# Reordering the start of a spectral-mixing and shrink kernel: early function table, copies first in the second unit, conversion and constant products in a gap

## Chip, cores, metric

One core of a Trainium2 chip. The metric is device time in microseconds (us) of one execution. Executions of the same kernel scatter by about 3 to 5 us on either side of the median, and the effects studied here are 1 to 12 us out of 2840. No run was slow by the record's rule (over 1.5% above the fastest of its kernel); one single look has no state. The experiments ran in three later calls on three chips, so runs of different calls are compared by their ratios to the kernel before, which ran in the same rounds. So most conclusions rest on two things together: the timed runs, and stretches of the trace between two fixed instructions, which repeat to a tenth of a us where nothing in them depends on DMA or on the clock.

## The reference

```python
# attention block: x (8, 3008, 256), filt_r, filt_i (1505, 256)
X = np.fft.rfft(x, axis=1)
y = np.fft.irfft(X * (filt_r + 1j * filt_i)[None], n=3008, axis=1)
# expert block on the 24064 x 256 result; w_in (256, 2048), w_out (2048, 256)
h = y.reshape(-1, 256) @ w_in
g = h - np.tanh(h)
out = g @ w_out
```

The weights arrive as 64-bit floats and are rebuilt as 32-bit floats with integer steps ("conversion" below).

## The kernel before

The Fourier transform is split over units of one or two batches. A prologue does unit 0 alone. The main loop then runs steps U = 0, 1, 2, ...: `up(U)` makes the seven products of a 2x2 block scheme with w_in (numbers 1 to 7 in `mm`), `shrink(U-1)` the activation on ScalarE and VectorE, `down(U-2)` the seven products with w_out; transforms of the next unit (`pf`, `pz`, `pe`) are strewn between. `pu` is the last product of a transform; ScalarE copies it to `ut`, and `up` works on `ut` and on `tu`, sums that GpSimd makes from it. The products of `up` go into three banks x, y, z (tiles that TensorE writes), those of `down` into four; a bank can be written anew once its copy is made. The program fixes the order by hand, and ScalarE's list in the prediction runs in it, so the order in this code is the order of each queue.

```python
def converted(tiles, src, dsts, queue, alone=False):      # one job: 128 x 512 numbers
    ...
    V.tensor_scalar(out=it, ...); V.tensor_scalar(out=pt, ...); V.tensor_scalar(out=st, ...)
    yield
    if alone:      # two steps on VectorE
        V.tensor_scalar(out=ft, ...); V.tensor_scalar(out=pt, ...)
    else:          # the same two on ScalarE
        ACT.activation(ft, it, AF.Identity, ...); ACT.activation(pt, pt, AF.Relu, bias=exp_b)
    yield
    ...            # three more steps and the writes of wu / wd, all on VectorE

# the prologue's end (tiles in the pools "pro" and "ps0", which are closed after it)
back0()                                   # last product pe and copy e1s, stored
for _ in range(EARLY): next(fs)           # two pf products, copies "a"
load_e2(*groups[0], e2s[0], slice(48, 64))
for _ in ws: pass                         # rest of quarters 3..5 of the weights
# ... then, in the main pools "dn" and "ps":
late = weights_slow(tiles1, range(6, 8))  # quarters 6 and 7 of the weights, inside the loop
for _ in last(0, z1): pass                # pu products, copies ut (a tile of "dn")

def up(U, d, e, s, t):      # d, e: steps of down; s: one of shrink; t: transforms, conversion
    mm(X, 1, True); mm(Y, 2, True)
    s1 = copied("s1")                     # ScalarE reads bank x
    t(0); d(); s()
    V.tensor_add(h[:, 0, :, 0:w], Y, s1)
    e(); s(); s(); t(1)
    mm(X, 6, False); mm(Z, 5, True)
    u2 = copied("u2")                     # ScalarE reads bank x; the next mm(X) waits for it
    d(); s(); e(); t(2)
    mm(X, 7, False)
    u3 = copied("u3")
    ...
# shrink: six steps: arctan+square, square with bias, end; the same for the other half
```

Of the kernel before, what the change touches and what calls it, by code (L numbers as in the profile page):

```python
# [9 lines left out]
F32 = mybir.dt.float32  # L10
# [4 lines left out]
AF = mybir.ActivationFunctionType  # L15
# [47 lines left out]
A, B = 0.18659689165196622, -0.6846325776203513  # L63
# [80 lines left out]
def kernel(  # L144
# [9 lines left out]
    nc = tc.nc  # L154
    V, G, ACT = nc.vector, nc.gpsimd, nc.scalar
# [11 lines left out]
    cst = ctx.enter_context(tc.tile_pool(name="cst", bufs=1))  # L167
# [97 lines left out]
    def begun(tiles, job, alone=False):  # L265
        j = converted(tiles, *job, nc.sync, alone)
        next(j)
        return j

    def weights(tiles, quarters, ahead):  # L270


        jobs = parts_of(quarters)
        began = [begun(tiles, job) for job in jobs[:ahead]]
        yield
        for k in range(len(jobs) + 1):
            if k < len(jobs):
                next(began[k])
            if k > 2 and k % 2:
                sums(quarters[k // 2 - 1])  # L280
            yield
            if k < len(jobs):
                next(began[k])
            if k > 0:
                for _ in began[k - 1]:
                    pass
            if k + ahead < len(jobs):
                began.append(begun(tiles, jobs[k + ahead]))
            yield
        sums(quarters[-1])  # L290
        yield

    def weights_alone(tiles, quarters):

        jobs = parts_of(quarters)
        began = [begun(tiles, job, True) for job in jobs[:2]]
        yield
        for k in range(len(jobs)):
            if k + 2 < len(jobs):
                began.append(begun(tiles, jobs[k + 2], True))  # L300
            for _ in began[k]:
                pass
            if k % 2:
                sums(quarters[k // 2])
            yield

    def weights_slow(tiles, quarters):

        jobs = parts_of(quarters)
        began = [begun(tiles, job) for job in jobs[:2]]  # L310
        yield
        for k in range(len(jobs)):
            for _ in began[k]:
                yield
            if k + 2 < len(jobs):
                began.append(begun(tiles, jobs[k + 2]))
            if k % 2:
                sums(quarters[k // 2])
                yield
# [212 lines left out]
    def up(U, d, e, s, t):  # L532

        i, u = divmod(U, 4)
        b, tu, w = uts[i]
        rhs = [b[0][0], b[1][0], b[1][1], tu[:, 3, 0:w], tu[:, 0, 0:w], tu[:, 1, 0:w],
               tu[:, 2, 0:w]]
        banks = {k: ps.tile([128, 2, 256], F32, tag=k, bufs=1, name=k) for k in "xyz"}
        X, Y, Z = (banks[k][:, :, 0:w] for k in "xyz")
        h = dn.tile([128, 4, 2, 256], F32, tag="h", bufs=3, name="h")  # L540
        hs[U] = (h, w)

        def mm(bank, q, first):
            for k in range(2):
                nc.tensor.matmul(bank[:, k], wu[:, q - 1, (2 * u + k) * 128:(2 * u + k + 1) * 128],  # L545
                                 rhs[q - 1], start=(first and k == 0), stop=True,
                                 skip_group_check=True)

        def copied(tag):
            t = dn.tile([128, 2, 256], F32, tag=tag, bufs=1, name=tag)[:, :, 0:w]  # L550
            ACT.copy(t, X)  # L551
            return t


        mm(X, 1, True)
        mm(Y, 2, True)
        s1 = copied("s1")
        t(0)
        d()
        s()  # L560
        V.tensor_add(h[:, 0, :, 0:w], Y, s1)  # L561
        e()
        s()
        s()
        t(1)
        mm(X, 6, False)
        mm(Z, 5, True)
        u2 = copied("u2")
        d()
        s()  # L570
        e()
        t(2)
        mm(X, 7, False)
        u3 = copied("u3")
        V.tensor_add(h[:, 3, :, 0:w], Z, u3)  # L575
        d()
        s()
        e()
        t(3)
        mm(X, 4, False)  # L580
        V.tensor_copy(h[:, 2, :, 0:w], X)  # L581
        s()
        d()
        e()
        t(4)
        mm(Z, 3, False)
        V.tensor_add(h[:, 1, :, 0:w], Z, u2)

    def shrink(U):

# [158 lines left out]
    def bounded(z):  # L749


        small = tr.tile([128, 2 * 4 * len(groups)], F32, tag="a2", bufs=2, name="small")
        ones = cst.tile([128, 1], F32, name="ones")
        least = cst.tile([128, 1], F32, name="least")
        G.memset(ones, 1.0)
        V.tensor_single_scalar(out=small, in_=y_sums, scalar=float(np.arctan(S * NEAR) ** 2),
                               op=ALU.is_lt)
        V.tensor_reduce(out=least, in_=small, axis=mybir.AxisListType.X, op=ALU.min)
        pc = z("pc", [1, 1])
        nc.tensor.matmul(pc, least, ones, start=True, stop=True)  # L760
        V.tensor_copy(count, pc)
# [69 lines left out]
    with tc.tile_pool(name="tr", bufs=2) as tr, tc.manual_schedule():  # L831
        with tc.tile_pool(name="pro", bufs=1) as pro, \
                tc.tile_pool(name="ps0", bufs=6, space=bass.MemoryType.PSUM) as ps0:

            def z0(name, shape):
                return ps0.tile(shape, F32, tag="z", bufs=6, name=name)
# [7 lines left out]
            def load_x0(c, cuts=(0, 8)):  # L844
                t = big([128, 8, DM], F32, "x0")
                for lo, hi in zip(cuts, cuts[1:]):
                    for h, rows, r, n in halves(0, 8 * c + lo, hi - lo):
                        (nc.sync, ACT)[h].dma_start(
                            t[rows, lo:lo + n, :],
                            dram(x.tensor, r * DM, [[NR * DM, 64], [1, n * DM]]))  # L850
                return t
# [60 lines left out]
            V.memset(near_b, B)  # L912
            V.memset(exp_b, -896.0)
            xs = [load_x0(0, (0, 4, 8)), load_x0(1), load_x0(2)]
            ws = weights_alone(tiles0, range(3))

            pad = pro.tile([64, DM], F32, name="pad")
# [48 lines left out]
            for j in range(NK // 2):  # L966
                c = j // 2
                if j % 2 == 0 and c + 1 < NK // 4:
                    if c + 2 < NK // 4:
                        a2[c + 2] = load_a2(0, c + 2, False, ("a2", "ft")[c % 2])  # L970
                        mats[c + 2] = load_slots(c + 2, pro)
                        fts[c + 2] = filters_of(c + 2)
                pz = z0("pz", [128, 2, DM])
                for i in range(2):
                    k = (2 * j + i) % 4
                    nc.tensor.matmul(pz[:, i], mats[c][0][0:R2, k],
                                     a2[c][0:R2, k * DM:k * DM + DM], start=True, stop=True)
                if waiting:
                    back0()
                uv = tr.tile([128, 2, DM], F32, tag="uv", bufs=2, name="uv")  # L980
                zs = tr.tile([128, 2, DM], F32, tag="zs", bufs=2, name="zs")
                ft = fts[c][:, :, j % 2 * 2:j % 2 * 2 + 2]
                V.tensor_mul(uv, pz, ft[:, 0])
                V.tensor_mul(zs, pz, ft[:, 1])
                waiting.append((j, uv, zs))
                next(ws, None)
                if j % 2 and c + 1 < NK // 4:
                    double_filters(fts[c + 1], c + 1)
                    turned(mats[c + 1][1], gx[(c + 1) % 2])
                if j == NK // 2 - 3:  # L990
                    fs = first(1, z1)
                    next(fs)
                if j == NK // 2 - 1:
                    e2s[0] = load_e2(*groups[0], None, slice(0, 48))
            back0()
            for _ in range(EARLY):
                next(fs)
            load_e2(*groups[0], e2s[0], slice(48, 64))
            for _ in ws:
                pass  # L1000


        with tc.tile_pool(name="dn", bufs=2) as dn, \
# [32 lines left out]
                                     [[2 * NK * DM, m], [DM, n], [1, DM]]), src)  # L1036
                    yield

            late, copies = weights_slow(tiles1, range(6, 8)), filters_d()
            total = 4 * len(groups)  # L1040
            for _ in last(0, z1):
                pass
# [1 line left out]
            for U in range(total + 2):  # L1044
# [27 lines left out]
                def d():  # L1072

                    next(dw, None)
# [5 lines left out]
                def s():  # L1080

                    next(sh, None)
# [26 lines left out]
                if U < total:  # L1109
                    if U == total - 1:  # L1110
                        one = tr.tile([128, 128], F32, tag="x", bufs=3, name="one_sb")
                        nc.sync.dma_start(one, one_d)
                    up(U, d, e, s, t)
                else:
                    for k in range(5):
                        s()
                        s()
                        d()
                        e()
                        t(k)  # L1120
                        if U == total + 1 and k == 0:
                            bounded(z1)
# [39 lines left out]
```

## Time and profile before

| | before |
|---|---|
| median of 6 runs | 2841.91 us (2837.63 to 2843.91) |
| span of the profiled run | 2839.5 us, granted clock 0.986 |
| TensorE busy | 96% of the span |
| TensorE busy from 114 to 170 us | 41.6 of 56 us |

The prediction shows the lines that matter: the slices, the windows from 114 to 222 us, TensorE's waits and ScalarE's queue in U=1. The windows' columns are start:end, length, busy us of TensorE, its weight loads, VectorE, ScalarE and GpSimd (with instruction counts), granted clock, share of the DMA engines, GB/s. In a timeline line the columns are start, duration, engine, line, operation, output<-inputs, sizes, count, and in brackets the idle time just before with what ended it.

### The profile page before, as it was taken

Reading aid. Unit: us, or ns where it says so; the run is one execution under the profiler, and the core shown is the slowest. Engines: PE = TensorE matmul, PEld = TensorE weight load, DVE = VectorE, ACT = ScalarE, POOL = GpSimd, SP = SyncE. Lnnn points to the kernel's source line nnn. Section 1 sums busy time; section 2 is a strip of 40 time slices with the busy share of each in tenths; the row PEclk is TensorE's granted clock in tenths of the full one; section 3 lists DMA queues with packets and bytes.
Section 4 is the critical chain, followed back from the end, with each engine's and each line's share of the span. In section 5 each row is a group of like instructions: output and inputs, shape, how many; then the busy total and the mean of one; then the engine's idle time right before and its main releaser. Section 6 shows DMA issues by size and latency. Waiting matters only on the chain.

```text
span 2839.5 us, 36615 instructions
## 1 busy us (share of the span) xinstructions
PE 2734.4 (96%) x12418; PEld 2270.6 (80%) x12418; DVE 1910.9 (67%) x2170; ACT 1881.9 (66%) x2794; POOL 1794.4 (63%) x1407
## 2 busy tenths in 40 slices
PE   4799999999999999999999999999999999999998
PEld 2567777988877787888877787788888888898887
DVE  6565665666766677656666776676676767677776
ACT  2476666666767766666666667666676676667665
POOL 5456887544677767744577776755466667656555
PEclk7899999999999999999999999999999999999999
DMA  9754443232233322232332223212222322101010
GB/s 251 199 184 104 116 107 85 69 104 72 67 80 77 79 70 60 48 90 79 73 94 67 70 71 79 54 41 65 63 65 61 79 55 53 34 17 27 16 22 17
DMA packets 322592, 217.53 MB, mean 77 GB/s; under 512 B 224782, under 2 KB 274746, under 8 KB 322156
## 3 DMA queue, kind: packets, MB, share of 16 engines
q1 hardware_dynamic: 266826, 157.28, 23.6%
q10 hardware_dynamic: 52818, 51.53, 6.0%
q0 software_dynamic: 2752, 6.30, 0.9%
q8 instruction: 100, 1.64, 0.3%
q14 instruction: 96, 0.79, 0.1%
HBM read 138.87 MB, written 79.17 MB: 77 GB/s over the span
## 4 chain that ended last, share of the span: by engine, by line
PE 77%; ACT 9%; issue 5%; DVE 4%; POOL 1%; ACTq 1%; DMA 0%; DVEq 0%; SPq 0%; POOLq 0%
PE o L653 31%; PE x L545 20%; PE z L545 9%; PE y L545 5%; PE pe L411 3%; PE pu L511 3%; ACT y L601 3%; PE pz L430 3%; PE pf L351 2%; DVE h L607 1%; ACT u L551 1%; ACT zs L444 1%; ACT y L602 1%; DVE uv L445 1%; ACT zs L443 1%
## 5 line engine op out<-in xcount | busy, mean ns | idle before, releaser
L653 PE MATMUL o<-t,wd 128*128 128x256 f32 (+2 forms) x3072 | 776.2, 375 | 1.8 <-POOL t L526 1.3
L607 DVE TENSOR_TENSOR h<-h,y 128x1024 f32<-128x1024 f32 (+2 forms) x384 | 570.4, 1485 | 279.6 <-ACT y L602 279.6
L653 PEld LDWEIGHTS o<-t,wd 128*128 128x128 f32 x3072 | 580.7, 190 | 74.2 <-POOL t L526 1.6
L545 PE MATMUL x<-tu,wu 128*128 128x256 f32 (+2 forms) x2304 | 589.1, 378 | 15.4 <-ACT u L551 15.1
L653 PE MATMUL o<-h,wd 128*128 128x256 f32 (+2 forms) x2304 | 582.4, 375 | 0.2 <-DVE h L611 0.2
L611 DVE SCALAR_TENSOR_TENSOR h<-sq,h 128x1024 f32<-128x1024 f32 (+2 forms) x384 | 566.7, 1476 | 20.5 <-ACT y L601 0.5
L524 POOL TENSOR_TENSOR t<-h 128x512 f32<-128x512 f32 (+2 forms) x192 | 240.6, 1253 | 501.6 <-DVE h L611 443.9
L545 PEld LDWEIGHTS x<-tu,wu 128*128 128x128 f32 x2304 | 427.8, 190 | 159.1 <-issue 73.1
L653 PEld LDWEIGHTS o<-h,wd 128*128 128x128 f32 x2304 | 431.2, 190 | 71.3 <-issue 18.8
L608 ACT ACTIVATE sq<-y,near_b 128x1024 f32<-128x1024 f32 (+2 forms) x384 | 435.6, 1134 | 5.0 <-DVE h L611 0.2
L601 ACT ACTIVATE y<-h 128x1024 f32<-128x1024 f32 (+2 forms) x384 | 400.0, 1042 | 14.8 <-ACT e L414 8.0
L602 ACT ACTIVATE y<-y 128x1024 f32<-128x1024 f32 (+2 forms) x384 | 399.2, 1040 | 12.2
L551 ACT COPY s<-x 128x512 f32<-128x512 f32 (+2 forms) x192 | 110.9, 577 | 443.2 <-PE x L545 431.7
L527 POOL TENSOR_TENSOR t<-t,h 128x512 f32<-128x512 f32 (+2 forms) x192 | 308.0, 1604 | 0.1
L551 ACT COPY u<-x 128x512 f32<-128x512 f32 (+2 forms) x384 | 219.2, 571 | 55.6 <-PE x L545 21.9
L525 POOL TENSOR_TENSOR t<-h,t 128x512 f32<-128x512 f32 (+2 forms) x192 | 241.3, 1257 | 15.1
L526 POOL TENSOR_TENSOR t<-h 128x512 f32<-128x512 f32 (+2 forms) x191 | 248.2, 1299 | 0.0
L575 DVE TENSOR_TENSOR h<-z,u 128x512 f32<-128x512 f32 (+2 forms) x192 | 129.5, 674 | 171.1 <-ACT u L551 168.2
L446 POOL TENSOR_TENSOR zs<-zs,ft 128x512 f32<-128x512 f32 x112 | 166.1, 1483 | 103.5 <-ACT zs L444 103.4
L447 POOL TENSOR_TENSOR uv<-uv,zs 128x512 f32<-128x512 f32 x112 | 213.7, 1908 | 14.0 <-DVE uv L445 5.5
L545 PE MATMUL x<-ut,wu 128*128 128x256 f32 (+2 forms) x768 | 199.2, 382 | 4.8 <-DVE h L581 3.0
L561 DVE TENSOR_TENSOR h<-y,s 128x512 f32<-128x512 f32 (+2 forms) x192 | 130.2, 678 | 106.0 <-PE y L545 87.7
(119 smaller groups left out, 3389.4 us busy)
## 6 DMA issues: line engine op xcount, KB each, us to landing
a<-ct SPq DMA_DIRECT2D x64, 384.0 KB, 4.2
ft<-filt SPq DMA_DIRECT2D x96, 256.0 KB, 4.3
out_dram<-ot SPq DMA_DIRECT2D x1392, 16.0 KB, 1.5
ct<-e ACTq DMA_DIRECT2D x112, 192.0 KB, 2.4
ct<-a ACTq DMA_DIRECT2D x80, 256.0 KB, 2.9
x_sb<-in_x_dram SPq DMA_DIRECT2D x69, 256.0 KB, 2.9
e<-ct SPq DMA_DIRECT2D x33, 512.0 KB, 4.3
fg<-fg SPq DMA_DIRECT2D x40, 392.0 KB, 6.2
```

What stands on the lines that cost most here:

```text
L524: G.tensor_sub(t[0], b[0][1], b[0][0])
L525: G.tensor_sub(t[1], b[1][1], t[0])
L526: (V if shared else G).tensor_sub(t[2], b[1][1], b[0][1])
L527: G.tensor_sub(t[3], t[1], b[1][0])
L545: nc.tensor.matmul(bank[:, k], wu[:, q - 1, (2 * u + k) * 128:(2 * u + k + 1) * 128], rhs[q - 1], start=(first and k == 0), stop=True, ski ...
L551: ACT.copy(t, X)
L601: ACT.activation(y[k], ht[k], AF.Arctan, scale=S)
L602: ACT.activation(y[k], y[k], AF.Square, accum_out=y_sums[:, 2 * U + k // 2:2 * U + k // 2 + 1])
L607: V.tensor_mul(ht[k], ht[k], y[k])
L608: ACT.activation(sq[k], y[k], AF.Square, bias=near_b, scale=A)
L611: V.scalar_tensor_tensor(out=ht[k], in0=sq[k], scalar=K, in1=ht[k], op0=ALU.add, op1=ALU.mult)
L653: nc.tensor.matmul(product(q), wd[:, q - 1, (2 * u + k) * 128: (2 * u + k + 1) * 128], rhs[q - 1][:, k], start=(u == 0 and k == 0 and q == ...
```

## The change

Its intent is to take out what TensorE waits for between the prologue and the steady loop. Five parts: (1) the function table for arctan loaded at the start; (2) in U=1 the copies u2 and u3 ahead of the shrink steps; (3) quarter 6 of the weights (the third of w_out's four) converted in the gap after the prologue, quarter 7 on VectorE alone; (4) ten constant products in the gap; (5) the vector of ones for the last check made ready early.

```diff
@@ weights_slow: all jobs with alone=True
-        began = [begun(tiles, job) for job in jobs[:2]]
+        began = [begun(tiles, job, True) for job in jobs[:2]]
@@ up: the fixed s() calls become shrinks(k), k = 0..7, after the same places
+        steps_at = ([1, 2, 0, 1, 0, 1, 1, 0] if U > 1 else [0, 0, 1, 0, 2, 0, 1, 2])
+        def shrinks(at):
+            for _ in range(steps_at[at]):
+                s()
   (places 2 and 4 are new: right after copy u2, and after copy u3 and its add)
@@ bounded
-        ones = cst.tile([128, 1], F32, name="ones")
-        G.memset(ones, 1.0)
@@ prologue
             xs = [load_x0(0, (0, 4, 8)), load_x0(1), load_x0(2)]
+            ACT.activation(near_b, near_b, AF.Arctan)
+            V.memset(near_b, B)
@@
                     fs = first(1, z1)
                     next(fs)
+                    ws_gap = weights(tiles0, range(6, 7), 2)
+                    next(ws_gap)
@@
-            for _ in ws:
-                pass
+            for w in (ws, ws_gap):
+                for _ in w:
+                    pass
+            warm = z0("warm", [128, 2, 128])
+            for _ in range(10):
+                nc.tensor.matmul(warm, wf1[:, 0], wf1, start=True, stop=True)
@@
-            late, copies = weights_slow(tiles1, range(6, 8)), filters_d()
+            late, copies = weights_slow(tiles1, range(7, 8)), filters_d()
@@ last unit
+                        ones = cst.tile([128, 1], F32, name="ones")
+                        G.memset(ones, 1.0)
```

More of the change, by code (lines that the diff above doesn't have):

```diff
@@ L315, in weights_slow @@
             if k + 2 < len(jobs):
-                began.append(begun(tiles, jobs[k + 2]))
+                began.append(begun(tiles, jobs[k + 2], True))
             if k % 2:
@@ L559, in up @@
         d()
-        s()
+        shrinks(0)
         V.tensor_add(h[:, 0, :, 0:w], Y, s1)
         e()
-        s()
-        s()
+        shrinks(1)
         t(1)
@@ L568, in up @@
         u2 = copied("u2")
+        shrinks(2)
         d()
-        s()
+        shrinks(3)
         e()
@@ L575, in up @@
         V.tensor_add(h[:, 3, :, 0:w], Z, u3)
+        shrinks(4)
         d()
-        s()
+        shrinks(5)
         e()
@@ L581, in up @@
         V.tensor_copy(h[:, 2, :, 0:w], X)
-        s()
+        shrinks(6)
         d()
@@ L587, in up @@
         V.tensor_add(h[:, 1, :, 0:w], Z, u2)
+        shrinks(7)
     def shrink(U):
```

## The prediction

> **What bounds the kernel now.** I read the 40 slices first, then a table of windows, then the per-engine timelines of the first 260 us.
>
> The slices:
>
> ```profile
> PE   4799999999999999999999999999999999999998
> PEclk7899999999999999999999999999999999999999
> ```
>
> TensorE is at 90% or more from the third slice of 71 us on, so the body is TensorE-bound and any time gained in front of it moves its start forward. Only the first two or three slices and the last have anything to gain. The windows between 114 and 222 us (start:end, length, then busy us of each engine, granted clock, DMA):
>
> ```profile
> 114.00:126.00 12.00, 5.36 (x20) 3.76 (x19) 1.19 (x3) 2.34 (x4) 0.73 (x1) 0.68 0.90 249
> 126.00:138.00 12.00, 10.89 (x39) 7.59 (x39) 4.68 (x10) 5.13 (x9) 2.86 (x4) 0.89 0.50 147
> 138.00:158.00 20.00, 14.50 (x43) 9.92 (x44) 12.50 (x19) 12.91 (x18) 5.16 (x6) 0.74 0.66 208
> 158.00:170.00 12.00, 10.81 (x45) 8.11 (x44) 9.48 (x14) 10.02 (x15) 5.29 (x6) 1.00 0.66 213
> 170.00:222.00 52.00, 52.00 (x227) 41.67 (x226) 33.75 (x43) 33.82 (x52) 29.55 (x29) 1.00 0.51 155
> ```
>
> From 114 to 170 us TensorE is busy 41.6 of 56 us, part of that at a clock of 0.68 to 0.89; from 170 on it is busy without a break. So the target of the change is those 56 us: the gap between prologue and main loop, and units U=0, 1, 2. Their waits on TensorE, from its timeline (start, duration, idle before it):
>
> ```profile
> 121.94 2.05 PE L511 MATMUL pu<-s_sb,e 128*128 128x128 f32 x8 [5.92 <-DMA e<-ct]
> 124.70 2.07 PE L511 MATMUL pu<-s_sb,e 128*128 128x128 f32 x8 [0.72 <-ACT ut L513]
> 126.57 1.91 PE L545 MATMUL x<-ut,wu 128*128 128x256 f32 x4
> 148.22 2.08 PE L545 MATMUL x<-tu,wu 128*128 128x256 f32 x4 [4.96 <-ACT u L551]
> 158.61 1.89 PE L653 MATMUL o<-h,wd 128*128 128x256 f32 x8
> 166.00 1.13 PE L545 MATMUL x<-tu,wu 128*128 128x256 f32 x4 [1.19 <-ACT u L551]
> ```
>
> Elsewhere the same eight pu instructions take 0.89 and four x instructions 0.86 us (chain of work, from 170 us on); here 2.07 and 1.71. These are half-clock matmuls after an idle. The 4.96 us wait belongs to U=1: the copy u2, which frees the x bank, stands on ScalarE behind this:
>
> ```profile
> 140.71 0.59 ACT L352 COPY a<-pf 128x512 f32<-128x512 f32 x1 [1.14 <-PE pf L351]
> 141.33 0.37 ACTq L353 DMA_DIRECT2D ct<-a  x1
> 141.74 0.63 ACT L216 ACTIVATE ft<-it 128x512 f32<-128x512 int32 x1 [0.44 <-ACT a L352]
> 142.28 0.70 ACT L217 ACTIVATE pt<-pt,exp_b 128x512 int32<-128x512 int32 x1
> 142.99 1.28 ACT L601 ACT_TABLE_LOAD   x1
> 144.28 1.06 ACT L601 ACTIVATE y<-h 128x1024 f32<-128x1024 f32 x1
> 145.37 1.06 ACT L602 ACTIVATE y<-y 128x1024 f32<-128x1024 f32 x1
> 146.55 1.15 ACT L608 ACTIVATE sq<-y,near_b 128x1024 f32<-128x1024 f32 x1
> 147.60 0.57 ACT L551 COPY u<-x 128x512 f32<-128x512 f32 x1
> ```
>
> Two conversions of w_out, the table load, arctan and two squares: all ahead of a copy that TensorE needs.
>
> **What the Trainium skill says.** "TensorE: Matmul & The Clock Gate", Part 1 (What's actually happening): the array falls to half clock after an idle window of about 3.4 us and needs about that much sustained work to come back. The trace agrees (idle 5.92 us, then 2.05 for 0.89), but an idle of 2.81 us is also enough: the pe matmuls at 255.54 us follow one and take 2.02 us. The same page, "Architectural detail", calls ScalarE and VectorE strict FIFO; the list above shows it. "ScalarE: Activation LUTs", What ACT_TABLE_LOAD costs: 1283 ns plus a drain of about 1380; Table sets: copy, relu and identity lie in every set. The trace has the 1283 ns twice (first copy at 3.42 us, first arctan at 142.99) and never again, though copies, identity, relu and square follow arctan; a drain it doesn't show. So one early arctan can serve the whole run.
>
> **The change part by part.**
>
> (1) The table. The dummy arctan sits where the first load stood (3.42 us; ScalarE's next work comes at 8.73), so it costs nothing there. It removes 1.28 us at 142.99.
>
> (2) Order in U=1. U=0 has no shrink, so only U=1 changes: u2 goes ahead of the first arctan, u3 ahead of the square sq. For u2 alone this takes 1.06+1.06+1.15 = about 3.3 us out of the wait.
>
> (3) Quarter 6 of w_out. Its two jobs leave U=0/1 for the gap, and quarter 7 takes their place in U=0/1 instead of U=2/3, with its two ScalarE steps (0.63+0.70, about 1.24 us net of overlap) on VectorE as two tensor_scalar steps (0.42 each by row L205, 0.9). So ScalarE loses 1.24 us twice in U=0/1 and twice in U=2/3; VectorE gains 0.9 twice in U=0/1 and loses about 3.9 us twice in U=2/3. In the gap: VectorE is free from 112.2 (last zs) to 123.15. Each job costs it three at 0.42, two more at about 0.69, one at 0.42 and three that make 0.83, i.e. 3.9 us. The ScalarE part can run from 117.4, after the two early pf copies, so the jobs end near 120.6 and 123.2; the four GpSimd sums (0.72 each) end near 126. GpSimd's tu for U=0 then comes about 127.6, and TensorE would want it at 127.1: some 0.5 us. The 1 MB of raw weights is issued at about 88 and 95 us, behind the x loads; DMA was full to 97 us, then at 0.3 to 0.4 until 116, so it lands before 112.
>
> (4) Ten constant products. 128x256 f32 is two instructions of 0.215 us: 4.3 us, from 116.0 (pf ends) to 120.3. The idle before pu shrinks from 5.92 to 1.6 us. pu itself starts no earlier: it waits for the chain copy (114.34), store, load (121.9). What they buy is the clock: pu 2 x (2.07-0.89), x 1.71-0.86, y 0.99-0.86.
>
> (5) ones. In the last 20 us TensorE waits for a memset queued on GpSimd behind t L527 (ends 2824.19). With it ready, the product waits only for VectorE's reduce (2823.23+0.55 = 2823.8). About 0.4 us, on the end's path.
>
> **Walking it through.** pu 121.94 to 122.85, copy ut to 123.5, second pu to 124.5 (before: 126.57). U=0: seven products and three pf at 0.86, 0.5 for tu and 0.85 for u3 (its ScalarE queue holds a pf copy and a DMA issue): U=1 starts at 134.4, before 137.8. So **-3.4 us** there. U=1: u2 done at 138.7, X7 139.6 to 140.5, pf to 141.3; arctan, square, a pf copy with its issue and u3 end at 142.6; the fourth product waits 1.35 us for it and z ends at 144.4. VectorE then does add, 1.2 and 1.2 us of shrink, and only then the copy that frees x, at 146.4: a second wait of 2.0 us. U=2 starts at 146.4 (before 156.0), and its first down product waits for the shrink of U=0 to end (149.6): 149.7 where it was 158.6, **-8.9 us**. In U=2 the 1.19 us wait at 166 goes, as ScalarE has 1.24 us less before u: **-10.1 us** at 166. From there TensorE is the bound and the shift is carried to the end. With (5): -10.5 us, 2830.3.
>
> I take back some for the clock. Between 141.3 and 146.4 I have 3.35 us idle in 5 us, which can throttle (0.6): U=2's first 4 us at half clock cost about 2.7 us, so 1.6 in the mean. The 1.6 us before pu could still throttle (0.2): 3.3 us, so 0.7. That leaves about -8.3 us: **2832.5 us**.
>
> **Rivals.**
>
> Moved wait: U=1 only trades its 4.96 us wait for one on VectorE and on the end of shrink 0, as in my own walk, and the clock falls again. For: shrink 0 needs about 5.6 us of ScalarE after U=0 has ended, and the down product can't start before. With both throttles the gain is about 5 us: 2836.
>
> Gap too full: the two jobs and sums hold up what follows. The main loop's tiles take over the memory of the prologue's, so the copy ut may wait for the last conversion at 123.2; and 1 MB more in a full DMA stretch could delay the last filters, for which TensorE already stands 5.25 us at 103.66 (GpSimd's turned copies end just then, after filter issues that wait for the DMA). Against: the raw loads queue behind what is needed sooner. If wrong by 2 to 4 us: 2836 to 2838.
>
> Hidden anyway: the body's other waits absorb the shift. Against: 52.00 of 52 us busy from 170 on, and the body's total waits for u are only 15.1 us in 27 places. If half were absorbed: 2835.5.
>
> Better than thought: no throttle at all, 2830; with VectorE out of the way in U=2, perhaps 2829.
>
> **Range and chances.** The repeat runs of before lie in 2838.8 to 2843.1, so 2 us of noise on each side. The best walk gives 2830, the rivals 2835 to 2838: the range is 2828.5 to 2838. A gain of 2% would be 57 us; all idle and slow-clock time from 114 to 170 us is some 22 us, so "faster" needs something that I don't see. Slower by 2% is as remote: at most a few us are added. Same: 0.985.
>
> **What would show it right or wrong.** One table load in the trace, near 3.4 us. Clock near 1.00 from 114 to 140 us and pu at about 0.95 us. No 4.96 us wait in U=1, but two shorter ones (for u3 and for the copy h L581) and a down product at about 150 us. No L216/L217 in the main loop. The pc product near 2823.8 minus the shift. Wrong if pu starts later than 122.5, if the wait at 103.66 grows, or if the products of U=2 run at half clock for longer than 5 us.

## The result

| | before | after |
|---|---|---|
| median of 6 runs | 2841.91 us | 2832.48 us (2830.20 to 2834.99) |
| span of the profiled run | 2839.5 us | 2831.1 us |
| granted clock | 0.986 | 0.990 |

Ratio 0.9969, 95% interval 0.9956 to 0.9982. A ratio is the mean time of one kernel's fast runs over that of the other's of the same rounds, so not quite the ratio of the medians. Twelve more runs of the changed kernel in a later call gave 2833.47 us and 0.9976 (0.9968 to 0.9985). So the gain is 6.5 to 9.5 us by the medians: 0.3%, the same within 2%.

The windows of the changed kernel, same bounds and columns as in the prediction:

```profile
114.00:126.00 12.00, 9.36 (x43) 7.88 (x42) 7.09 (x15) 4.65 (x8) 4.38 (x6) 0.87 0.87 244
126.00:138.00 12.00, 11.07 (x42) 7.68 (x42) 8.40 (x19) 4.03 (x8) 2.45 (x4) 0.99 0.54 166
138.00:158.00 20.00, 17.08 (x68) 12.37 (x67) 13.44 (x16) 16.68 (x25) 9.90 (x10) 1.00 0.67 216
158.00:170.00 12.00, 12.00 (x56) 9.53 (x55) 6.55 (x8) 7.28 (x11) 6.38 (x6) 1.00 0.62 193
```

TensorE is busy 49.5 of the 56 us (41.6 before), and from 126 us on the clock stays at 0.99 or more. The first window, though, has 0.87: not all is mended there. TensorE's timeline of the changed kernel shows where:

```profile
112.20 1.88 PE L351 MATMUL pf<-x_sb,wf_sb 128*128 128x512 f32 x4
113.92 4.48 PE L1018 MATMUL warm<-wf_sb 128*128 128x256 f32 x20
118.58 1.13 PE L511 MATMUL pu<-s_sb,e 128*128 128x128 f32 x8 [0.17 <-DMA e<-ct]
122.17 1.57 PE L511 MATMUL pu<-s_sb,e 128*128 128x128 f32 x8 [2.47 <-ACT ut L513]
123.53 1.91 PE L545 MATMUL x<-ut,wu 128*128 128x256 f32 x4
...
141.88 1.13 PE L351 MATMUL pf<-x_sb,wf_sb 128*128 128x512 f32 x2 [0.92 <-ACT a L352]
...
146.70 1.13 PE L545 MATMUL x<-ut,wu 128*128 128x256 f32 x4 [1.79 <-DVE h L590]
...
149.76 1.99 PE L663 MATMUL o<-h,wd 128*128 128x256 f32 x8 [0.21 <-DVE h L621]
```

The first pu now runs at full clock (1.13 where it took 2.05), right behind the constant products. Then comes a **new wait of 2.47 us for the copy ut**, and x runs at half clock again (1.91; 1.03 at full clock). In U=1 the 4.96 us wait is gone; two of 0.92 and 1.79 us stand in its place, and the first down product comes at 149.76 (158.61 before). ScalarE's queue in U=1 shows why: u2 is ahead of the arctan, no table load and no conversion stand between them.

```profile
138.64 0.59 ACT L551 COPY u<-x 128x512 f32<-128x512 f32 x1 [0.49 <-DVE ft L219]
139.12 1.06 ACT L611 ACTIVATE y<-h 128x1024 f32<-128x1024 f32 x1
140.21 1.06 ACT L612 ACTIVATE y<-y 128x1024 f32<-128x1024 f32 x1
```

For comparing runs I cut the start into stretches between fixed instructions of TensorE: the first pf of the prologue's end; the first pu; the first x of U=1 (X1); the third x of U=2, the one that waited at 166.00 before (X7). All in us, one profile each:

| kernel | first pf at | pf to pu | pu to X1 | X1 to X7 |
|---|---|---|---|---|
| before | 114.14 | 7.80 | 15.88 | 28.18 |
| before, second profile | 115.13 | 7.31 | 16.41 | 28.44 |
| walk in the prediction | 114.14 | 7.80 | 12.5 | 21.5 |
| after | 112.20 | 6.38 | 16.09 | 21.23 |
| after, second profile | 114.45 | 6.60 | 14.79 | 21.23 |

So U=1 and U=2 went as walked, to a few tenths; the stretch from pu to X1 did not gain what it should; and pf to pu gained about 1 us that nobody had predicted. For the second profile of the changed kernel I had expected 16.1 us from pu to X1, as in the first; 14.79 was a miss: the wait for ut came again (2.25 us), but not the half clock behind it. From X7 to the end all profiles of this study take 2670 to 2675 us. The two of before are 3.2 us apart (2673.5 and 2670.3), and the two of the changed kernel (2675.2 and 2673.7) are 2.6 us longer in the mean, so no absorption shows beyond the scatter.

At the end of the run, TensorE waits for the product with ones. Before, from the timeline:

```profile
2824.28 0.19 PE L760 MATMUL pc<-ones,least 128*1 128x1 f32 x2 [2.40 <-POOL ones L755]
```

After:

```profile
2815.69 0.19 PE L768 MATMUL pc<-ones,least 128*1 128x1 f32 x2 [1.95 <-DVE least L766]
```

The releaser changes from GpSimd's memset to VectorE's reduce, and the wait is 0.45 us shorter, as part (5) had it (0.4). No run has this part alone.

### The profile page after: what moved, and what is told of

The parts are those of the page before. It is cut to its first block, busy times and chain, and to the rows that moved or that the text cites. A ratio compares the mean times of both kernels' runs of the same rounds, so it can differ in the third digit from the quotient of the medians.

```text
span 2831.1 us, 36652 instructions
## 1 busy us (share of the span) xinstructions
PE 2730.9 (96%) x12438; PEld 2269.8 (80%) x12438; DVE 1911.7 (68%) x2175; ACT 1878.5 (66%) x2790; POOL 1792.0 (63%) x1407
## 4 chain that ended last, share of the span: by engine, by line
PE 78%; ACT 9%; issue 5%; DVE 5%; DMA 2%; POOL 1%; ACTq 1%; SPq 0%; DVEq 0%; POOLq 0%
PE o L663 31%; PE x L545 20%; PE z L545 9%; PE y L545 6%; PE pe L411 3%; PE pu L511 3%; ACT y L611 3%; PE pz L430 3%; PE pf L351 2%; DVE h L617 1%; ACT u L551 1%; ACT zs L444 1%; DVE uv L445 1%; ACT y L612 1%; ACT zs L443 1%
```

## The experiments

The theory after the result: the order in U=1, the early table and the emptied ScalarE queue are worth what was predicted; the constant products are worth theirs only if nothing else holds pu and x; and the conversions moved into the gap hold the copy ut. The rivals: the order only trades waits; the constant products buy nothing; ut waits for the raw weights of quarter 7, which the profile names as its releaser.

**1. Old order in U=1.**

```diff
-        steps_at = ([1, 2, 0, 1, 0, 1, 1, 0] if U > 1 else [0, 0, 1, 0, 2, 0, 1, 2])
+        steps_at = [1, 2, 0, 1, 0, 1, 1, 0]
```

> The changed kernel with the old order of shrink steps in unit U=1. Theory (the prediction's part 2): u2 stands behind arctan, square and sq again, so TensorE waits some 2.4 us for it in U=1 (4.96 us before, less the 1.28 us table load and 1.24 us of conversion), and perhaps falls to half clock after it; U=1 takes 14 to 15 us in place of 12.0, and the run is 1.5 to 3.5 us longer than the changed kernel. Rival (the order only trades one wait for another, as shrink 0 sets the pace anyway): within 0.5 us of the changed kernel.

Measured: 2835.48 us (21 runs), ratio to before 0.9983 (0.9977 to 0.9990), against 0.9969 and 0.9976 of the changed kernel. X1 to X7 24.44 us, 3.2 more than the changed kernel. TensorE's timeline of this run has the expected wait:

```profile
143.06 1.36 PE L545 MATMUL x<-tu,wu 128*128 128x256 f32 x4 [2.42 <-ACT u L551]
145.67 2.08 PE L351 MATMUL pf<-x_sb,wf_sb 128*128 128x512 f32 x2 [1.25 <-ACT a L352]
```

2.42 us for u2, as worked out (2.4), another 1.25, then half clock (2.08 for pf). The order is no mere trade: it is worth 3.2 us here by the trace, and 2 to 4 by the ratios, whose intervals overlap.

**2. Without the constant products.**

```diff
-            warm = z0("warm", [128, 2, 128])
-            for _ in range(10):
-                nc.tensor.matmul(warm, wf1[:, 0], wf1, start=True, stop=True)
```

> The changed kernel without its ten constant products. The prediction's part 4 said they buy about 3.3 us of clock: then this is 3 us longer than the changed kernel. The trace of the changed kernel speaks for less: the first pu runs at full clock, but the copy ut then starts only at 121.53 though pu ended at 119.7, and the second pu and the first x run at half clock again. If that wait is set by something else than pu, the first pu may take 2.05 us and end at 120.6 without any harm, and this is within 0.7 us of the changed kernel.

Measured: 2833.03 us (13 runs), ratio 0.9977 (0.9969 to 0.9986). Pu to X1 is 16.25 us, 0.16 more than in the first profile of the changed kernel and 1.5 more than in its second. So in the changed kernel the ten products buy between nothing and 1.5 us, as the clock falls behind them or not: both profiles have a wait of over 2 us for ut there (2.47 and 2.25), and after it the clock fell once and stayed up once. In the profiles of experiments 1 and 3, which have the ten products too, it fell after waits of 2.07 and 2.10 us. The timed runs can't tell the difference (0.9977 against 0.9969 and 0.9976).

**3. Without the early table.**

```diff
-            ACT.activation(near_b, near_b, AF.Arctan)
-            V.memset(near_b, B)
```

> The changed kernel without the early arctan. Two table loads in the trace. Theory: the load falls into U=1 after the copy u2, in front of the first arctan, and shrink 0 paces U=1 and U=2, so the first down product comes 1.3 us later and the run is about 1.3 us longer than the changed kernel. Rival: it hides beside TensorE's work in U=1, 0.

Measured: 2833.12 us (17 runs), ratio 0.9977 (0.9970 to 0.9984). X1 to X7 22.64, 1.41 us more than the changed kernel. The table load of 1.28 us is on the path as predicted. The timed runs can't tell 1.4 us from nothing (0.9977 against 0.9969 and 0.9976).

**4. The gap's conversions on VectorE alone.**

```diff
-                    ws_gap = weights(tiles0, range(6, 7), 2)
+                    ws_gap = weights_alone(tiles0, range(6, 7))
```

> The changed kernel with the two conversions in the gap wholly on VectorE, so that they don't wait for the pf copies on ScalarE and end some 2.5 us sooner (about 118.7 where the last product ended at 121.3). Theory: the copy ut waits for the last of the conversions, as the main loop's tiles take over the memory of the prologue's; then ut starts right after pu (within 0.2 us), the second pu, the first x and y run at full clock, the wait of 2.47 us shrinks to 0.7, and the run is 3 to 4 us shorter than the changed kernel (some 2828.5). Rival: ut waits for the raw weights of quarter 7, whose landing the trace names; then ut starts at the same time after the e2 load is issued (5.9 us) and the run is the same as the changed kernel.

Measured: 2830.24 us (6 runs), ratio 0.9966 (0.9954 to 0.9978). Pu to X1 12.75 us: 3.3 less than in the first profile of the changed kernel, 2.0 less than in the second. The ratios put the gain at 1 to 3 us, with intervals that overlap, so the evidence is the trace. From VectorE's and ScalarE's timelines of this run:

```profile
119.46 0.83 DVE L230 SCALAR_TENSOR_TENSOR wd<-conv 128x256 f32<-128x256 f32 x3
123.23 0.43 DVE L204 TENSOR_SCALAR it<-raw 128x512 int32<-128x512 int32 x1 [2.95 <-DMA raw<-in_moe_w_out_dram]
```

```profile
121.61 0.59 ACT L513 COPY ut<-pu 128x512 f32<-128x512 f32 x1 [5.48 <-PE pu L511]
```

The last conversion ends at 120.29, pu ends at 121.53, and ut starts 0.08 us after it, at 121.61, **before** the raw weights of quarter 7 land (VectorE waits for them until 123.23). The rival falls. In the changed kernel the same two views read:

```profile
120.47 0.83 DVE L230 SCALAR_TENSOR_TENSOR wd<-conv 128x256 f32<-128x256 f32 x3
```

```profile
121.53 0.59 ACT L513 COPY ut<-pu 128x512 f32<-128x512 f32 x1 [3.67 <-DMA raw<-in_moe_w_out_dram]
```

The conversion ends at 120.47 + 0.83 = 121.30 and ut starts 0.23 us later. In all five profiles of kernels with this form of the gap (after twice, experiments 1 to 3) it is 0.23 us, though the whole moves by 2 us between them. The releaser that the line names was merely the last event near. Counted from the first pf, ut starts after 9.33 us in all five, whenever pu came (6.4 to 6.8 us after pf): as long as the conversions end last, an earlier pu wins nothing. Why ut waits for conversions whose results it doesn't use, the program suggests: ut lies in a pool opened where the prologue's pool, with the conversions' scratch tiles, has been closed, so it may take over their memory. That reading of the memory I did not test; that the end of the conversions is what counts is shown.

**5. The constant products alone, on the kernel before.**

```diff
             for _ in ws:
                 pass
+            warm = z0("warm", [128, 2, 128])
+            for _ in range(10):
+                nc.tensor.matmul(warm, wf1[:, 0], wf1, start=True, stop=True)
```

> The kernel before with the ten constant products in the gap and nothing else of the change. No conversion stands in the gap here, so the copy ut follows pu at once. The prediction's part 4 taken by itself: both pu, x and y of U=0 run at full clock, the first x of U=1 comes 2.0 to 3.3 us sooner after the first pu than before (15.88 us there, so 12.6 to 13.9), and the run is 2 to 3.3 us shorter than before. Rival (the products buy nothing, the clock falls again after them): x of U=1 at 15 us or later after pu, time as before.

Measured: 2836.78 us (21 runs), ratio 0.9988 (0.9981 to 0.9995), about 3.4 us shorter. Pu to X1 13.16 us, 2.7 and 3.2 less than in the two profiles of before. From TensorE's timeline of this run:

```profile
125.46 1.16 PE L511 MATMUL pu<-s_sb,e 128*128 128x128 f32 x8 [0.72 <-ACT ut L513]
126.45 1.03 PE L545 MATMUL x<-ut,wu 128*128 128x256 f32 x4
```

1.16 and 1.03 us where before had 2.07 and 1.91. Part (4) was sized rightly (3.3); what failed was its meeting with part (3).

**6. Experiment 4 without the constant products.** The two edits of experiments 2 and 4 together.

> The version with the gap's conversions on VectorE, without the constant products. Theory: with the wait for the conversions gone the products are worth what the prediction said: without them pu, pu, x and y run at half clock, the first x of U=1 comes some 2 to 3.3 us later after the first pu than the 12.75 us of the version with them (so 14.8 to 16), and the run is 2 to 3.3 us longer. In the changed kernel itself taking them out cost only 0.16 us of this stretch. Rival: they are worth nothing here either: 13.0 us or less.

Measured: 2833.20 us (9 runs), ratio 0.9975 (0.9965 to 0.9985). Pu to X1 15.04, 2.3 us more than in experiment 4; the products are worth 2.3 us by the trace, and 2.6 by the ratios (0.0009 of 2840), whose intervals overlap. With the wait gone they have their worth.

**7. The quarter back in the loop.**

```diff
-                    ws_gap = weights(tiles0, range(6, 7), 2)
-                    next(ws_gap)
@@
-            for w in (ws, ws_gap):
-                for _ in w:
-                    pass
+            for _ in ws:
+                pass
@@
-            late, copies = weights_slow(tiles1, range(7, 8)), filters_d()
+            late, copies = weights_slow(tiles1, range(6, 8)), filters_d()
```

> The changed kernel with quarter 6 of w_out back in the main loop (as quarter 7, on VectorE alone); all else of the change stays. Theory, from the version with the gap's conversions on VectorE: the conversions in the gap are what holds the copy ut, so without them ut follows pu, the clock stays up, and the first x of U=1 comes 12.8 to 13.2 us after the first pu (16.1 and 14.8 in the two profiles of the changed kernel). On the other side two more jobs of about 4.7 us stand on VectorE in U=2 and U=3, which costs 0 to 1 us from the first x of U=1 to the third x of U=2 (21.2 in the changed kernel). So this stretch is 1 to 3 us shorter in sum than in the changed kernel: the gap part by itself loses there. Rival (the prediction's part 3): the gap part gains 1.2 us in U=2 and costs nothing before; then this is 1 us longer. The first pf is expected at 114 to 116 us, as in the two profiles without the gap's early raw loads, against 112.0 to 114.5 in the eight with them; if it comes at 113 or sooner, that difference was chance.

Measured: 2832.55 us (11 runs), ratio 0.9975 (0.9966 to 0.9984): the same as the changed kernel. Pu to X1 12.75, the same as in experiment 4; X1 to X7 22.42, 1.2 us more than the changed kernel, a little over the 0 to 1 that I gave, as the first down product waits for VectorE (1.22 us). Pf to pu is 7.64. The gap part as written gives 1.2 us in U=2, takes 2 to 3.3 before it, and gains some 1 us from pf to pu: in sum nothing (from the first pf to X7 42.8 us here, 43.7 and 42.6 in the changed kernel).

**8. The order alone, on the kernel before.** The new `steps_at` and `shrinks` calls and nothing else.

> The kernel before with the new order in U=1 and nothing else. Taken from the changed kernel less this part (3.2 us in the profile from the first x of U=1 to the third x of U=2), the order is worth 3 to 5 us by itself: from the first x of U=1 to the third x of U=2 23 to 25.5 us, where before has 28.2. The table load (1.28 us) and the conversion's two ScalarE steps (1.24 us) still stand in U=1, the table load now behind u2. Rival: with them left, the order alone only moves the wait: 27 us or more. The first pf as in the profiles without early raw loads, 114 to 116 us.

Measured: 2839.39 us (13 runs), ratio 0.9998 (0.9990 to 1.0007). X1 to X7 25.11 us, 3.1 less than before and within what I expected; the time is at most 2.8 us shorter by the interval, and about 0.5 by its middle. The two don't agree. In the profiled run the prologue was late (first pf at 117.95, the latest of all profiles), which eats the gain there. But that run was the slowest of the 13 (2842.67 us), so its lateness can't stand for the others. Why their time is so little shorter stays open. The worth of the order rests on experiment 1.

**9. The kernel before once more**, one look.

> The kernel before once more, for a second profile: the first pf at 114 to 116 us if the early raw loads have a part in its time, spread over 112 to 116 us like the others if it is chance; from the first pf to the first pu 7.6 to 7.8 us if it belongs to the order of the loads, 6.4 to 7.1 if that is chance too. The stretch from pu to the third x of U=2 44.1 us as in the first profile.

Measured: 2839.48 us; the stretches are in the table above. Pu to X7 is 44.85 us, 0.8 more than in the first profile; y of U=0 took 1.73 us in place of 1.20, so the half clock lasted longer. Pf to pu took 7.31 us, in neither of the two ranges that I had named for order and for chance. With this, the first pf lies at 113.9 to 118.0 us in the five profiles without early raw loads (before twice, experiments 5, 7, 8) and at 112.0 to 114.5 in the eight with them, ranges that overlap; pf to pu takes 7.3 to 7.8 and 6.4 to 7.1. The second pair of ranges doesn't overlap: with the quarter in the gap, the way from pf to pu is shorter by about 0.9 us. Whether its raw loads or its conversions do this was not tested apart. The last load before pu is issued 3.4 us after pf in either kind (3.9 and 4.1 in experiments 1 and 3); from its issue to pu it is 3.9 to 4.4 us without the early raw loads and 2.7 to 3.7 with them. Why it lands sooner was not found.

**10. A better version.** Experiment 4, and in U=1 the first arctan of shrink 0 right behind s1:

```diff
-        steps_at = ([1, 2, 0, 1, 0, 1, 1, 0] if U > 1 else [0, 0, 1, 0, 2, 0, 1, 2])
+        steps_at = ([1, 2, 0, 1, 0, 1, 1, 0] if U > 1 else [0, 0, 1, 0, 1, 1, 2, 0])
@@
         s1 = copied("s1")
+        if U == 1:
+            s()
         t(0)
@@
-                    ws_gap = weights(tiles0, range(6, 7), 2)
+                    ws_gap = weights_alone(tiles0, range(6, 7))
```

> The version with the gap's conversions on VectorE, and in U=1 the first arctan of shrink 0 directly behind the copy s1, its square step behind u2, its end behind the copy u3, the second arctan ahead of the third pf. Theory: TensorE's waits in U=1 and before the first down product are the length of shrink 0's chain on ScalarE and VectorE, which begins only at u2 in the changed kernel (139.1 us) though its data are there at 134.6. Begun some 2.5 us sooner, the first x of U=2 and the first down product come about 2 us sooner: from the first x of U=1 to the first down product 13 us in place of 15.2, and the run is 2 us shorter than the version with the conversions on VectorE alone. Rival: u2 comes later for it and TensorE waits there for as much as it gains: 15 us, same time.

Measured: 2828.51 us (5 runs), ratio 0.9956 (0.9942 to 0.9969), some 12.5 us under before and 5.0 under the median of the changed kernel in the same call. From X1 to the first down product 13.63 us (15.20 in experiment 4; I had said 13), and X1 to X7 is 19.84, 1.5 us less than there. I had said 2 us for the run; the ratios of the two (0.9956 and 0.9966, two calls) differ by about 3 us, but their intervals overlap. TensorE's timeline:

```profile
140.38 1.13 PE L351 MATMUL pf<-x_sb,wf_sb 128*128 128x512 f32 x2 [0.39 <-ACT a L352]
...
144.14 1.13 PE L545 MATMUL x<-ut,wu 128*128 128x256 f32 x4 [0.73 <-DVE h L592]
...
146.87 1.99 PE L665 MATMUL o<-h,wd 128*128 128x256 f32 x8
```

The waits are 0.39 and 0.73 where they were 0.92 and 1.79, and the down product no longer waits. The step after the changed kernel's order was to see that, once the copies are first, it is shrink 0's chain that paces U=1.

## Why the prediction was right, and where it wasn't

The number was right to a microsecond (2832.5 predicted, 2832.48 and 2833.47 measured), but not every step of it: two errors, of 1 to 2 and of 2.3 us, cancelled, so it is luck that it fell so near.

- **Table (part 1): right.** One load in the trace, at 3.4 us. 1.28 predicted, 1.41 by experiment 3.
- **Order (part 2): right.** 3.3 predicted, 3.2 by experiment 1; two shorter waits came about where the walk put them (first x of U=2 at 146.4 predicted, 146.70 measured; down product 149.7 and 149.76). The second is for the copy h, as said. The first is not for u3 at the fourth product (1.35 us in the walk): it stands just before that product, at a pf that waits 0.92 us for the copy a. Those absolute times agree partly by luck, as the stretches show. The rival "moved wait" was half true: two smaller waits came, as walked, and experiment 10 shows that they could be cut further.
- **Quarter in the gap (part 3): half wrong.** What it frees in U=2 was right: X1 to X7 21.5 predicted, 21.23 measured. The failing step is "so the jobs end near 120.6 and 123.2", left without a consequence for ut in the walk, where pu was given as the only thing before it. I had named the danger under the rival "gap too full", with the memory as the cause, and given it no share of the mean. It cost 2.0 to 3.3 us from pu to X1 (experiment 4), or 1.6 to 2.6 counted from the first pf (22.5 and 21.4 us to X1, against 19.8). The jobs ended 9.1 us after the first pf, just as the walk had them: by its own numbers ut would have waited some 0.6 us, and as pu came earlier it waited 1.8 (pu ended at 119.71, ut started at 121.53).
- **Constant products (part 4): right in size, wrong in place.** 3.3 predicted, 2.7 to 3.2 in the stretch and about 3.4 in time when alone (experiment 5), but 0.2 to 1.5 beside the conversions (experiment 2). With part 3's wait this is why "-3.4 us there" turned out as +0.2 and -1.1 from pu to X1.
- **Ones (part 5): right**, 0.4 and 0.45.
- **Clock: over-priced in U=2, under-priced at pu.** I took back 1.6 us for a fall of the clock in U=2 that no profile shows with waits of 0.92 and 1.79 us there, and 0.7 for one before pu; the fall came after pu instead. (The price of 2.7 us for "4 us at half clock" doesn't come out either: half clock loses half its length, so 2.7 us lost are some 5.4 us of it, as in the kernel before from 150.83 us on.)
- **Not foreseen:** pf to pu shorter by about 1 us with the quarter in the gap. In the changed kernel this won nothing, as ut came 9.33 us after pf all the same. Counted from the first pf, X1 was walked at 20.3 us and came at 22.5 and 21.4 (23.7 before). So 1.1 to 2.2 us are missing there, and the 2.3 us taken back for the clock made up for them.
- **Hidden anyway: not seen.** Half absorbed would be about 5 us. From X7 to the end the changed kernel is 2.6 us longer in the mean of two profiles, less than the 3.2 us between the two of before.
- **Signs and readings.** Of the signs, "Clock near 1.00 from 114 to 140 us" failed (0.87 in the first 12 us). None of the "wrong if" came: pu started at 118.58 and 121.05, the wait at 103.66 shrank from 5.25 us to 1.84 and 3.22, and U=2 ran at full clock. Two readings were loose: TensorE is busy without a break from 170 to 222 us only (the prediction itself names an idle of 2.81 us later), and ScalarE's list has two steps of one conversion, not two conversions.

## What to carry to other kernels

When work is moved into a gap, ask what is released at its end besides the data: here the next phase's first tile could not be written before the moved work was done, and the idle that this made undid the clock that another part of the change had bought. On an in-order engine put the copies that free a bank first, and then look again, as the chain behind them becomes the pace. And when a sum comes out right, check its terms: two of these were off by 1 to 2.3 us, with opposite signs.

## What the Trainium skill lacked or had wrong

- "TensorE: Matmul & The Clock Gate", Part 1, gives an idle window of about 3.4 us before the clock falls (and says in "A second HAM failure mode", without a length, that frequent short idles made it fall in one kernel). Here a wait of 2.47 us in the first profile of the changed kernel was followed by half clock (x at 1.91 us), as were 2.07 and 2.10 us in experiments 1 and 3, and one of 2.25 us at the same place in its second profile was not (x at 1.03). An idle well below 3.4 us may cost the clock or not, in one and the same program.
- The same page has no word on filler products in a gap. Ten of them (4.48 us of TensorE) kept the clock and were worth 2.7 to 3.2 us in the stretch and about 3.4 us in time when nothing else held TensorE behind them (experiment 5).
- "ScalarE: Activation LUTs", What ACT_TABLE_LOAD costs, adds a drain of about 1380 ns to the 1283 ns. No drain shows here: the load started at 142.99 us and the arctan at 144.28, and taking the load off the path gave 1.41 us.
- No page that I read says that, where one pool is closed and the next opened, a tile's first write can wait for work whose results it doesn't use; here the copy ut started 0.23 us after the last such instruction in five profiles of five. That the memory is the reason was not tested.
